# Pooled attention and a low-rank MLP on one core: a pair's remainders turned at once, outputs scaled on ScalarE, two adds a head given to GpSimd

## The chip, the cores and the metric

One core of one Trainium2 chip runs the whole program. The metric is the device time of one execution in microseconds. Three runs of the kernel before gave 885.32, 886.49 and 887.59 us, so the median is 886.49 us.

## The reference

The inputs are q, k and v of shape (4 batches, 8 heads, 1152 tokens, 64 columns) in float32, and the weights U, V, w_ch1 and w_ch2.

```
q_pool = q.reshape(B, H, S // 2, 2, D).mean(axis=3)          # 576 queries a head
scores = q_pool @ k^T / sqrt(D);  scores -= max over keys
attn   = exp(scores);  attn /= (sum over keys + 1e-09)
x      = attn @ v, heads side by side                        # (4, 576, 512)
h      = x^T @ U @ V        # along the tokens, rank 32
u      = x + h^T
out    = u + relu(u @ w_ch1) @ w_ch2                          # 512 -> 2048 -> 512
```

## The kernel before

There are 32 heads, numbered n = 8 b + h. The program does not write its instructions in their final order. It hands each piece of work to a planner (`Plan`, line 43) with a due time, the engines that may do it with a price in nanoseconds for each, and what it reads and writes. The planner runs a list schedule of its own prices: on each engine it takes the earliest due piece among those that can start soon enough (`SLACK`), and writes every engine's instructions in the order that comes out. On the chip each engine works through its own list in order. A piece with two engines (`dual`, line 399) goes to the one on which the planner sees it end first. VectorE pieces marked `port`, and all GpSimd pieces, are planned one after the other, and a link (line 1153) makes a GpSimd piece wait for the last VectorE piece of that kind.

A head goes through these steps, all in `head` (line 510). The pairs of query rows are added, turned and put in `Q1` and, for what the first rounding left, in `Q2`. The keys are turned into `T1`; a DMA copies T1 into `T2` and a row of ones lies beside it. Scans (line 696) multiply queries and keys once for a bound of each block's maximum, which VectorE reduces (line 702); the result is turned, negated and sent into a row of `Q2` by a DMA (line 731). Then the scores are computed again in the other orientation (lines 756 and 757), with keys in partitions: nine key blocks `j`, in three PSUM banks `s`. ScalarE takes the exponential of each bank into a unit of `big` (line 763). VectorE or GpSimd adds the units into `acc` (line 739): eight adds a head, seven in batch 0, whose last unit is summed by TensorE. TensorE multiplies the units with v into a bank of `m` (line 788), whose partitions 0 to 63 and 64 to 127 hold the head's outputs for the first and second 288 queries. Five banks `m` are shared by all that is not a score.

Every second head ends a pair. Each head's outputs are copied by ScalarE to `ay` (line 796), the pair's sums are formed by products with ones (line 779) and copied to `sr` (line 802). TensorE turns them by 128x128 products with an identity: three turns of the sums (line 825), four of the outputs' first 256 columns (`t4`) and two for the remaining 32 columns of each head, taken as the last 128 columns (`t2`, line 812). VectorE adds 1e-9 to the sums (line 828), takes reciprocals (line 832), multiplies the remainders into `XH` (line 835, two instructions) and the rest into `X` (line 839, one instruction of 512 columns).

After a batch's last head its `tail` (line 844) does the token mix and the MLP. Its products (lines 996, 1111 and 1040) are placed between the work of the next batch's heads, and after the last head TensorE does nothing else. In batch 0 there is no earlier MLP to place; while its heads run and after them, the weights are decoded (lines 430 to 438 and 920 to 923).

Of the kernel before, what the change touches and what calls it, by code (L numbers as in the profile page):

```python
# [9 lines left out]
F32 = mybir.dt.float32  # L10
# [3 lines left out]
AF = mybir.ActivationFunctionType  # L14
ALU = mybir.AluOpType
# [219 lines left out]
def kernel(  # L235
# [32 lines left out]
    FG = 2  # L268
    QT, KS = -9.86, -10.51
    LEAD = 52820.1, 7258.73  # L270
    WHOLE_KEYS, SPLIT = (False, False, True, True), 8
# [6 lines left out]
    LOOSE = (1, 0, 0, 0)  # L278
    SQUARES, SMALL = (False, False, True, True), 2.0
    APART = (True, True, False, False)  # L280
# [5 lines left out]
    SCALE = 0.5 / float(D) ** 0.5  # L286
    HEAD0, HEAD = 16770.0, 20724.3
    SLOT = HEAD / NG
    MLP_START, MLP_RATE = 5.082, (2.2, 2.197, 2.107, 2.2)
    DEC_START, DEC_LEAD = 98276.3, 12248.1  # L290
    SLACK = 18.29
    BIAS, BIAS_FROM = -300.0, 0.0
# [28 lines left out]
    def cut(of, first, n, shape, rows=P):  # L321
# [20 lines left out]
        acc=slots("acc", 3, [P, NQ]),  # L342
        ay=slots("ay", 2, [P, 2, HALF]),
        mp=slots("mp", 2, [P, 15]),
        mx=slots("mx", 2, [P, 5], F32R),
        mr=slots("mr", 2, [5, P], F32R),
        sr=slots("sr", 2, [P, HALF]),
        sm=slots("sm", 2, [P, 2, NS]),
# [50 lines left out]
    def dual(n, f):  # L399
        return {"dve": (v_(n), lambda: f(nc.vector)), "pool": (g_(n), lambda: f(nc.gpsimd))}  # L400
# [4 lines left out]
    def dma(nbytes):  # L405
        return nbytes / RATE

    def setup():
        nc.vector.memset(C["uh"][0].tile[:, 0, 0:2 * P].bitcast(F32), 1.0)
        make_identity(nc, ident)  # L410
        nc.vector.tensor_copy(identr, ident)
        for i in range(2):
            nc.gpsimd.memset(C["T2"][i].tile[D:D + 1].bitcast(F32), 1.0)
            nc.gpsimd.memset(C["mp"][i].tile, -3.0e38)
        nc.vector.memset(Vst[:, 0:PAD].bitcast(F32), 0.0)
        nc.gpsimd.memset(C["qb"][0].tile.bitcast(F32), 0.0)
# [93 lines left out]
    def head(n):  # L510
# [3 lines left out]
        T = lambda G: begin(n) + G * (SLOT if n >= NWHOLE else SLOT * HEAD0 / HEAD)  # L514
        whole = WHOLE_KEYS[b] and not SQUARES[b]
        kt, qt, vt, qp = (new(c) for c in ("k", "q", "v", "qp"))
        ks = None if whole else new("k" if SQUARES[b] else "ks")
        T1, T2, T3, Q1, Q2, qb, acc, mp = (new(c) for c in ("T1", "T2", "T3", "Q1", "Q2", "qb", "acc", "mp"))
        odd = h % 2
        if not odd:  # L520
            pair[:] = [new(c) for c in ("ay", "sr", "sm", "rs")] + [[], []]
        ay, sr, sm, rs, accs, summed = pair
        squares = SQUARES[b]
        if squares:
# [107 lines left out]
        if squares:  # L632
            kr = lambda: kt.t.rearrange("p j (x d) -> p (j x) d", d=32)
            kq = lambda: ks.t.rearrange("p j d -> p (j d)")
            for z in range(2):
                for c in range(2):
                    a = 32 * (2 * z + c)
                    op(T(-17), ("sp", SMALL * dma(73728), lambda a=a, z=z, c=c: nc.sync.dma_start(
                        kr()[a:a + 32], k[b, h, z * S // 2:(z + 1) * S // 2, 32 * c:32 * c + 32].rearrange("(m p) d -> p m d", p=32)), 0, 1200, BULK), go, [(kt, a)])
# [9 lines left out]
            t1, t3 = half_(0) + half_(1), [(T3, 0)]  # L649
            op(T(-6), ("act", 500, lambda: nc.scalar.dma_start(T2.t[0:D].bitcast(F32), T1.t[0:D].bitcast(F32)), 3300), [(T1, 0, 0), (T1, 1, 0)],  # L650
               [(T2, p_, z) for p_ in range(2) for z in range(2)])
# [10 lines left out]
        else:  # L662
# [19 lines left out]
            op(T(-6 if n else -20), way(lambda: que.dma_start(T2.t[0:D].bitcast(F32), T1.t[0:D].bitcast(F32)), 294912, 3300), t1, [(T2, p_, z) for p_ in range(2) for z in range(2)])  # L682
        op(T(-10), ("sp", dma(2 * 294912), lambda: nc.sync.dma_start(
# [54 lines left out]
        def add(at, a, b_, r):  # L738
            op(at, dual(NQ, lambda e: e.tensor_tensor(acc.t, a(), b_(), op=ALU.add)), r, [acc])  # L739

        for j in range(NJ):
            if j % 2 == 0:
                pair_ = j + 1 < NJ
                pu[j] = new("p2" if pair_ else "p1")
                if pair_:
                    pu[j + 1] = pu[j]
                    todo = [((j, j + 1), 0, NARROW, j), ((j,), NARROW, NQ, j + 0.9), ((j + 1,), NARROW, NQ, j + 1.493)]
                else:
                    todo = [((j,), 0, HALF, j), ((j,), HALF, NQ, j + 0.5)]
                for js, qa, qz, when in todo:  # L750
# [31 lines left out]
        for j0, j1 in GV[b]:  # L782
            last = j1 == NJ and odd and not APART[b]

            def value(js=range(j0, j1), last=last):
# [9 lines left out]
               [(vt, 0)] + keys(range(j0, j1)) + (summed if last else []), [pa] + ([pk] if last else []))  # L795
        op(T(NJ + AV), ("act", a_(HALF, True), lambda: nc.scalar.activation(ay.t[:, odd], pa.t[:, 0:HALF], AF.Copy)), [pa], [(ay, odd)])  # L796

        if not odd:
            return
        if APART[b]:  # L800
            op(T(NJ + AV), ("pe", parts * 4 * (HALF / 2.4 + 1.0) + TOT, total, TSL), summed, [pk])
        op(T(NJ + AV), ("act", a_(HALF, True), lambda: nc.scalar.activation(sr.t, pk.t[:, 0:HALF], AF.Copy)), [pk], [sr])

        first = (0, P, HALF - P)
        E = NJ + AV + YT
        pq, py, pz = new("m"), new("m"), new("m")
# [12 lines left out]
        def t2():
            for e in range(2):  # L820
                turn(e, HALF - P, pq.t[:, e * P:(e + 1) * P])

        def t3():
            for t, c0 in enumerate(first):
                nc.tensor.transpose(pz.t[:, t * P:(t + 1) * P], sr.t[:, c0:c0 + P], ident)

        op(T(E), ("pe", 3 * TP, t3), [sr], [pz])
        op(T(E + 0.1), ("dve", 80, lambda: nc.vector.tensor_scalar_add(
            sm.t, pz.t[:, 0:3 * P].rearrange("p (c e x) -> p e c x", e=2, x=32)[:, :, :, 0], 1e-9)), [pz], [sm])
        op(T(E), ("pe", 2 * TP, t2), [(ay, e) for e in range(2)], [pq])  # L830
        op(T(E), ("pe", 4 * TP, t4), [(ay, e) for e in range(2)], [py])
        op(T(E), ("dve", 135, lambda: nc.vector.reciprocal(rs.t, sm.t)), [sm], [rs])
        last = slice(P - 32, P)
        for f in range(2):
            op(T(E + 0.3), ("dve", v_(P) + 105, lambda f=f: nc.vector.tensor_tensor(
                XH[b].t[hb + 32 * f:hb + 32 * f + 32, cs].rearrange("p (e d) -> p e d", e=2),
                pq.t[last, 0:2 * P].rearrange("p (e f d) -> p f e d", e=2, f=2)[:, f],
                rs.t[last, :, 4 + f:5 + f].to_broadcast([32, 2, D]), op=ALU.mult)), [pq, rs], [(XH[b], b, h // 2, f)])
        op(T(E + 0.3), ("dve", v_(512), lambda: nc.vector.tensor_tensor(
            X[b].t[:, :, cs].rearrange("p t (e d) -> p t e d", e=2), py.t.rearrange("p (e t d) -> p t e d", e=2, d=D),  # L840
            rs.t[:, :, 0:4].rearrange("p e t -> p t e").unsqueeze(3).to_broadcast([P, 4, 2, D]), op=ALU.mult)),
           [py, rs] + (over if h > 1 else []), [(X[b], h // 2)] + (over if h == 1 else []))

    def tail(b, clock):
# [343 lines left out]
```

## Time and profile before

| | |
|---|---|
| median of the three runs | 886.49 us |
| profiled execution, its own time | 885.24 us |
| its span, first to last instruction | 883.1 us |
| TensorE busy | 872.8 us (99%) |
| VectorE busy | 751.9 us (85%) |
| ScalarE busy | 502.4 us (57%) |
| GpSimd busy | 218.8 us (25%) |

The profile shows one execution. Busy time of an engine is the time in which at least one of its instructions runs. Matmuls overlap and their ends are modelled, so a busy TensorE need not be at its peak. Two instructions that follow at once on VectorE or ScalarE overlap a little too. The chain that ended last follows the end of the program back to what released each step.

### The profile page before, as it was taken

The numbers are of one execution on the slowest core, as the hardware profiler recorded it, in microseconds if no ns is written. First come the engines' busy times: TensorE is split into PE (matmuls) and PEld (weight loads), VectorE is DVE, ScalarE is ACT, GpSimd is POOL, SyncE is SP. The second block draws the span as 40 slices with busy tenths as digits, with TensorE's granted clock in tenths as the row PEclk, the third lists the DMA queues.
The fourth block names the chain that finished last, engine by engine and source line by source line (L and its number), as shares of the span: only waits on it lengthen the run. The fifth ranks groups of instructions, "written<-read, shape, count | busy, mean of one in ns | idle before, by whom it ended". The sixth has DMA issues, their size and how long they took to land.

```text
span 883.1 us, 15648 instructions
## 1 busy us (share of the span) xinstructions
PE 872.8 (99%) x5469; PEld 710.0 (80%) x5469; DVE 751.9 (85%) x1494; ACT 502.4 (57%) x1094; POOL 218.8 (25%) x220
## 2 busy tenths in 40 slices
PE   9999999999999999999999999999999999999998
PEld 8777777687777777779888878888887788899987
DVE  8999999989999999997797889888884553898885
ACT  6788889767777777755454556455554221422220
POOL 2233332334344354550112122101130000111110
PEclk9999999999999999999999999999999999999999
DMA  5244364455657564883544545535442255455432
GB/s 171 80 125 147 90 180 142 130 170 191 220 165 223 167 156 135 225 209 89 150 105 100 140 94 126 126 80 149 112 146 85 96 184 195 173 193 190 167 104 100
DMA packets 146324, 128.73 MB, mean 146 GB/s; under 512 B 100907, under 2 KB 119110, under 8 KB 146246
## 3 DMA queue, kind: packets, MB, share of 16 engines
q1 hardware_dynamic: 143622, 118.47, 45.5%
q10 hardware_dynamic: 2624, 9.28, 4.4%
q8 instruction: 43, 0.70, 0.3%
q14 instruction: 35, 0.29, 0.1%
HBM read 96.17 MB, written 21.50 MB: 133 GB/s over the span
## 4 chain that ended last, share of the span: by engine, by line
PE 87%; DVE 8%; DMA 2%; ACT 2%; issue 1%; SPq 0%; ACTq 0%; DVEq 0%
PE m L1111 21%; PE m L996 15%; PE m L788 14%; PE s L756 7%; PE s L757 7%; PE m L696 7%; PE s L1040 6%; DVE mp L702 3%; DVE acc L739 1%; PE m L779 1%; DMA room<-mr 1%; PE m L812 1%; PE m L962 1%; PE m L669 1%; PE m L698 1%
## 5 line engine op out<-in xcount | busy, mean ns | idle before, releaser
L763 ACT ACTIVATE big<-s 128x320 f32<-128x320 f32 (+2 forms) x448 | 203.4, 479 | 127.0 <-PE s L757 124.2
L702 DVE TENSOR_REDUCE mp<-m 128x1 f32<-128x384 f32 (+1 forms) x448 | 216.2, 532 | 25.7 <-PE m L696 24.6
L1111 PE MATMUL m<-w,hh 128*128 128x512 f32 x798 | 223.9, 395 | 0.0
L996 PE MATMUL m<-rest,w 128*128 128x512 f32 (+1 forms) x768 | 186.1, 353 | 0.0
L756 PE MATMUL s<-room 128*128 128x256 f32 (+2 forms) x576 | 167.5, 302 | 0.7 <-ACT big L763 0.4
L757 PE MATMUL s<-room 65*128 65x256 f32 (+2 forms) x576 | 164.9, 298 | 1.8 <-DMA room<-mr 1.8
L1111 PEld LDWEIGHTS m<-w,hh 128*128 128x128 f32 x798 | 144.0, 188 | 23.1 <-ACT ay L796 0.5
L788 PE MATMUL m<-big,v 128*64 128x288 f32 x1152 | 148.5, 410 | 0.3 <-DVE mp L702 0.3
L996 PEld LDWEIGHTS m<-rest,w 128*128 128x128 f32 x768 | 132.8, 189 | 14.0 <-issue 1.4
L739 DVE TENSOR_TENSOR acc<-acc,big 128x576 f32<-128x576 f32 x162 | 125.2, 773 | 8.8 <-ACT big L763 6.8
L788 PEld LDWEIGHTS m<-big,v 128*64 128x64 f32 x1152 | 79.2, 137 | 58.7 <-issue 3.9
L696 PE MATMUL m<-room 128*128 128x384 f32 x384 | 125.6, 358 | 0.6 <-DVE mp L702 0.2
L756 PEld LDWEIGHTS s<-room 128*128 128x128 f32 x576 | 108.9, 189 | 13.0 <-issue 4.8
L757 PEld LDWEIGHTS s<-room 65*128 65x128 f32 x576 | 108.9, 189 | 8.3 <-issue 1.6
L739 POOL TENSOR_TENSOR acc<-acc,big 128x576 f32<-128x576 f32 x54 | 77.0, 1427 | 68.3 <-DVE acc L739 16.9
L696 PEld LDWEIGHTS m<-room 128*128 128x128 f32 x384 | 68.5, 188 | 19.5 <-DVE mp L702 4.7
L1115 DVE TENSOR_TENSOR X<-m,X 128x512 f32<-128x512 f32 x95 | 64.3, 681 | 12.0 <-PE m L1111 11.6
L438 POOL TENSOR_TENSOR wt<-wt,rx 128x512 int32<-128x512 int32 (+2 forms) x35 | 44.3, 1266 | 95.5 <-ACT big L763 20.7
L1002 DVE SCALAR_TENSOR_TENSOR hh<-m,hh 128x512 fp32r<-128x512 f32 (+1 forms) x64 | 37.4, 584 | 32.2 <-ACT hh L1000 31.8
L1000 ACT ACTIVATE hh<-m 128x512 fp32r<-128x512 f32 (+1 forms) x64 | 32.9, 514 | 52.3 <-PE m L996 51.6
L584 POOL CAST qb<-room 64x64 fp32r<-64x64 f32 x50 | 16.4, 329 | 135.4 <-DVE acc L739 42.0
L394 ACT ACTIVATE room<-m 64x288 fp32r<-64x288 f32 (+1 forms) x109 | 46.3, 438 | 2.0 <-PE m L570 0.5
(137 smaller groups left out, 1055.8 us busy)
## 6 DMA issues: line engine op xcount, KB each, us to landing
w<-wc SPq DMA_DIRECT2D x96, 512.0 KB
rx<-in_moe_w_ch_dram SPq DMA_DIRECT2D x32, 512.0 KB
wc<-w SPq DMA_DIRECT2D x32, 512.0 KB
v<-in_v_dram SPq DMA_DIRECT2D x32, 288.0 KB
room<-room ACTq DMA_DIRECT2D x31, 288.0 KB
q<-in_q_dram SPq DMA_DIRECT2D x16, 288.0 KB
k<-in_k_dram SPq DMA_DIRECT2D x64, 72.0 KB
q<-in_q_dram SPq DMA_DIRECT2D x128, 36.0 KB
```

The costliest lines, as they stand in the source:

```text
L394: ways = {"act": (a_(n, True) + hold, lambda: f(lambda o, i: nc.scalar.activation(o, i, AF.Copy)), far)}
L696: nc.tensor.matmul(pm.t[:, 0:w], Q1.t[:, t * P - 64:t * P + 64], T1.t[:, cs_], start=True, stop=True)
L702: op(T(MX0 + 0.3 + MXS * u / 14), ("dve", v_(w), lambda c=c, t=t, w=w, pm=pm: nc.vector.reduce_max(mp.t[:, c * 5 + t:c * 5 + t + 1], pm.t[ ...
L739: op(at, dual(NQ, lambda e: e.tensor_tensor(acc.t, a(), b_(), op=ALU.add)), r, [acc])
L756: nc.tensor.matmul(o, T1.t[:, kc], Q1.t[:, qa:qz], start=True, stop=False)
L757: nc.tensor.matmul(o, T2.t[:, kc], Q2.t[:, PAD + qa:PAD + qz], start=False, stop=True)
L763: op(T(when + 0.1), ("act", a_(len(js) * nq, True), lambda js=js, qa=qa, qz=qz, nq=nq, ss=ss, p=pu[j], e=js[0] % 2: nc.scalar.activation(p ...
L788: nc.tensor.matmul(pa.t[hf * D:(hf + 1) * D, 0:HALF], vt.t[:, j], pu[j].t[:, j % 2, hf * HALF:(hf + 1) * HALF], start=(j == 0), stop=(j == ...
L996: op(now, ("pe", mm(nb), lambda c=c, i=i, a=a, bb=bb, w=w, ph=ph, sl=sl: nc.tensor.matmul(ph.t[:, 0:nb], w.t[:, a, c * P:(c + 1) * P], (ul ...
L1040: nc.tensor.matmul(bank.t[:, 0:NB], left(a, c), ub.t[:, i, bb, c], start=(c == 0 and j == 0), stop=(c == 1 and j == 2))
L1111: op(now, ("pe", mm(512), lambda f=f, i=i, a=a, bb=bb, w=w, h_=h_: nc.tensor.matmul(po.t, h_.t[:, a, ns], w.t[:, bb], start=(f == fg and i ...
L1115: op(now, ("dve", v_(512), lambda: nc.vector.tensor_tensor(x(), po.t, x(), op=ALU.add)), [po], bk[t])
```

## The change

For each pair, `ay` becomes one row of 864 columns: the first 256 columns of head 0, of head 1 and of the sums, then the last 32 columns of each of the three. ScalarE copies each of the three sources in two pieces (`keep`). Seven turns follow: two for the sums and one for all three remainders at once (`t3`), and four for the outputs (`t4`). The added 1e-9 takes three instructions for one, and the multiplications of the remainders become four pieces of 64 columns that may go to ScalarE or VectorE. In batches 0 and 1 (`SCALED`) the rest of the outputs is scaled on ScalarE, two pieces of four activations with a scale for each partition, in place of one VectorE multiplication. In heads 0 to 15 (`GIVEN`) the adds of units 1 and 2 go to GpSimd and all others to VectorE. `SQUARES` changes its form only: it held for batches 2 and 3 and now holds from head 16. Several due times and promised landing times move.

```diff
-    QT, KS = -9.86, -10.51
-    LEAD = 52820.1, 7258.73
+    QT, KS = -9.86, -10.14
+    LEAD = 68186.1, 7053.71
+    SCALED = (True, True, False, False)
+    SQUARES, SMALL = 16, 2.0
+    GIVE, GIVEN = (1, 2), 16
-    HEAD0, HEAD = 16770.0, 20724.3
+    HEAD0, HEAD = 16680.3, 20724.3
-    MLP_START, MLP_RATE = 5.082, (2.2, 2.197, 2.107, 2.2)
-    DEC_START, DEC_LEAD = 98276.3, 12248.1
-    SLACK = 18.29
+    MLP_START, MLP_RATE = 5.082, (2.2, 2.197, 2.131, 2.099)
+    DEC_START, DEC_LEAD = 80776.6, 12248.1
+    SLACK = 16.65
-        ay=slots("ay", 2, [P, 2, HALF]),
+        ay=slots("ay", 2, [P, 6 * P + 96]),
-        sr=slots("sr", 2, [P, HALF]),
+        for x in C["sm"]:
+            nc.gpsimd.memset(x.tile, 1.0)
...
-  k's loads of batches 2 and 3:  ... .rearrange("(m p) d -> p m d", p=32)), 0, 1200, BULK), go, [(kt, a)])
+  k's loads of batches 2 and 3:  ... .rearrange("(m p) d -> p m d", p=32)), 0, 1800, BULK), go, [(kt, a)])
-  both copies of T1 into T2:     ... nc.scalar.dma_start(T2.t[0:D].bitcast(F32), T1.t[0:D].bitcast(F32)), 3300)
+  both copies of T1 into T2:     ... nc.scalar.dma_start(T2.t[0:D].bitcast(F32), T1.t[0:D].bitcast(F32)), 4300)
...
         def add(at, a, b_, r):
-            op(at, dual(NQ, lambda e: e.tensor_tensor(acc.t, a(), b_(), op=ALU.add)), r, [acc])
+            ways = dual(NQ, lambda e: e.tensor_tensor(acc.t, a(), b_(), op=ALU.add))
+            if n < GIVEN:
+                ways = {"pool": ways["pool"]} if j in GIVE else {"dve": ways["dve"]}
+            op(at, ways, r, [acc], port=True)
...
-                    todo = [((j, j + 1), 0, NARROW, j), ((j,), NARROW, NQ, j + 0.9), ((j + 1,), NARROW, NQ, j + 1.493)]
+                    todo = [((j, j + 1), 0, NARROW, j), ((j,), NARROW, NQ, j + 0.8295), ((j + 1,), NARROW, NQ, j + 1.493)]
-                    todo = [((j,), 0, HALF, j), ((j,), HALF, NQ, j + 0.5)]
+                    todo = [((j,), 0, HALF, j), ((j,), HALF, NQ, j + 0.3653)]
...
-        op(T(NJ + AV), ("act", a_(HALF, True), lambda: nc.scalar.activation(ay.t[:, odd], pa.t[:, 0:HALF], AF.Copy)), [pa], [(ay, odd)])
+        def keep(e, src):
+            op(T(NJ + AV), ("act", a_(2 * P, True), lambda: nc.scalar.activation(ay.t[:, 2 * e * P:2 * (e + 1) * P], src.t[:, 0:2 * P], AF.Copy)), [src], [(ay, e)])
+            op(T(NJ + AV), ("act", a_(32, True) + 16, lambda: nc.scalar.activation(
+                ay.t[:, 6 * P + 32 * e:6 * P + 32 * (e + 1)], src.t[:, 2 * P:HALF], AF.Copy)), [src], [(ay, "last", e)])
+        keep(odd, pa)
...
-        op(T(NJ + AV), ("act", a_(HALF, True), lambda: nc.scalar.activation(sr.t, pk.t[:, 0:HALF], AF.Copy)), [pk], [sr])
+        keep(2, pk)
-        pq, py, pz = new("m"), new("m"), new("m")
+        py, pz = new("m"), new("m")
...
         def t3():
-            for t, c0 in enumerate(first):
-                nc.tensor.transpose(pz.t[:, t * P:(t + 1) * P], sr.t[:, c0:c0 + P], ident)
+            for i in range(2):
+                turn(4 + i, pz.t[:, i * P:(i + 1) * P])
+            nc.tensor.transpose(pz.t[0:96, 2 * P:3 * P], ay.t[:, 6 * P:], ident)
-        op(T(E), ("pe", 2 * TP, t2), [(ay, e) for e in range(2)], [pq])
+        for e in range(2):
+            op(T(E + 0.1), ("dve", 110, lambda e=e: nc.vector.tensor_scalar_add(
+                sm.t[32 * e:32 * e + 32, 0, 4:6], pz.t[64:96, 2 * P:3 * P].rearrange("p (f e x) -> p e f x", e=2, x=32)[:, e, :, 0], 1e-9)),
+               [pz], [(sm, e)])
...
         for f in range(2):
-            op(T(E + 0.3), ("dve", v_(P) + 105, lambda f=f: nc.vector.tensor_tensor(... pq, rs ...)), [pq, rs], [(XH[b], b, h // 2, f)])
+            for e in range(2):
+                op(T(E + 0.3), {
+                    "act": (a_(D, True) + MOVE, lambda to=to, fr=fr, by=by: nc.scalar.activation(to(), fr(), AF.Copy, scale=by())),
+                    "dve": (v_(D) + 105, lambda to=to, fr=fr, by=by: nc.vector.tensor_scalar(to(), fr(), by(), None, op0=ALU.mult)),
+                }, [pz, rs], [(XH[b], b, h // 2, f, e)])
+        if SCALED[b]:
+            for e in range(2):
+                def scaled(e=e):
+                    for t in range(4):
+                        nc.scalar.activation(X[b].t[:, t, (h - 1 + e) * D:(h + e) * D], py.t[:, 2 * e * P + t * D:2 * e * P + (t + 1) * D], AF.Copy, scale=rs.t[:, e, t:t + 1])
+                op(T(E + 0.3), ("act", 4 * (a_(D, True) + 16), scaled), [py, rs] + (over if h > 1 else []), [(X[b], h // 2, e)] + (over if h == 1 and e == 1 else []))
+        else:
+            the VectorE multiplication of 512 columns as before
```

## Rows read from the trace of the kernel before

**Rows 1.** The page: busy time of each engine, and tenths in 40 slices.

```profile
PE 872.8 (99%) x5469; PEld 710.0 (80%) x5469; DVE 751.9 (85%) x1494; ACT 502.4 (57%) x1094; POOL 218.8 (25%) x220
...
PE   9999999999999999999999999999999999999998
...
DVE  8999999989999999997797889888884553898885
ACT  6788889767777777755454556455554221422220
```

**Rows 2.** The page: shares of the chain that ended last, by engine.

```profile
PE 87%; DVE 8%; DMA 2%; ACT 2%; issue 1%; SPq 0%; ACTq 0%; DVEq 0%
```

**Rows 3.** Stages: us, busy (x instructions) of PE, PEld, DVE, ACT, POOL, clock, DMA.

```profile
19.40:140.20 120.80, 119.75 (x887) 90.90 (x886) 115.78 (x255) 100.36 (x236) 38.89 (x43) 1.00 0.45 127
140.20:178.30 38.10, 35.98 (x249) 26.03 (x242) 37.61 (x74) 31.97 (x73) 10.42 (x9) 1.00 0.44 133
178.30:332.20 153.90, 152.82 (x920) 119.71 (x919) 144.29 (x283) 112.31 (x239) 66.44 (x54) 1.00 0.62 187
332.20:700.00 367.80, 366.13 (x2363) 300.70 (x2362) 306.97 (x596) 201.65 (x438) 80.80 (x81) 1.00 0.50 127
700.00:883.00 183.00, 179.97 (x921) 155.48 (x919) 131.57 (x255) 44.54 (x87) 15.71 (x16) 1.00 0.47 163
```

**Rows 4.** The chain within 19.4 to 140.2 us, shares by line.

```profile
by line: PE m L788 23.1%; PE s L756 13.3%; PE s L757 12.4%; PE m L696 12.0%; DVE mp L702 7.5%; DVE acc L739 4.8%; ACT room L394 3.6%; issue 2.9%; PE m L669 2.8%; PE m L779 2.5%; DMA room<-mr 2.0%; PE m L698 1.6%; PE m L812 1.6%; ACT big L76
```

**Rows 5.** Timelines and chain: start us, us, engine, line, what, count: dense TensorE work.

```profile
61.79 0.28 PE L756 MATMUL s<-room 128*128 128x256 f32 x1
61.91 0.29 PE L757 MATMUL s<-room 65*128 65x256 f32 x1
62.03 0.69 PE L696 MATMUL m<-room 128*128 128x384 f32 x3
62.56 0.31 PE L756 MATMUL s<-room 128*128 128x320 f32 x1
62.70 0.31 PE L757 MATMUL s<-room 65*128 65x320 f32 x1
62.85 0.34 PE L696 MATMUL m<-room 128*128 128x384 f32 x1
...
24.05 3.06 PE m L788 x24
...
49.82 0.27 PE L812 MATMUL m<-ident,ay 128*128 128x128 f32 x1
...
697.16 0.60 PE L812 MATMUL m<-ident,ay 128*128 128x128 f32 x4
```

**Rows 6.** ScalarE's forms: count, busy us, mean ns of one, idle before.

```profile
L796 ACT ACTIVATE ay<-m 128x288 f32<-128x288 f32 x32 | 13.2, 411 | 41.6 <-PE m L788 41.5
L939 ACT ACTIVATE room<-m 128x256 fp32r<-128x256 f32 x5 | 1.9, 378 | 0.0
L938 ACT ACTIVATE room<-m 128x128 fp32r<-128x128 f32 x5 | 1.4, 278 | 4.8 <-PE m L962 4.8
```

**Rows 7.** Line 739's adds by stage: us, busy (x) of DVE, of POOL.

```profile
0.00:140.00 140.00, 37.71 (x50) 8.51 (x6) 1.00 0.46 131
140.00:332.00 192.00, 33.07 (x43) 30.02 (x21) 1.00 0.58 176
```

**Rows 8.** Forms of VectorE and GpSimd: count, busy us, mean ns of one.

```profile
L835 DVE TENSOR_TENSOR XH<-m,rs 32x128 f32<-32x128 f32 x32 | 9.4, 295 | 1.1
L839 DVE TENSOR_TENSOR X<-m,rs 128x512 f32<-128x512 f32 x12 | 8.3, 691 | 0.4
L828 DVE TENSOR_SCALAR sm<-m 128x12 f32<-128x12 f32 x16 | 2.6, 160 | 7.5 <-PE m L825 7.5
L936 DVE TENSOR_TENSOR wt<-m,wt 128x128 f32<-128x128 f32 x15 | 3.4, 279 | 0.0
L739 POOL TENSOR_TENSOR acc<-acc,big 128x576 f32<-128x576 f32 x54 | 77.0, 1427 | 68.3 <-DVE acc L739 16.9
```

More of the change, by code (lines that the diff above doesn't have):

```diff
@@ L278 @@
     LOOSE = (1, 0, 0, 0)
-    SQUARES, SMALL = (False, False, True, True), 2.0
+    SCALED = (True, True, False, False)
+    SQUARES, SMALL = 16, 2.0
+    GIVE, GIVEN = (1, 2), 16
     APART = (True, True, False, False)
@@ L514, in head @@
         T = lambda G: begin(n) + G * (SLOT if n >= NWHOLE else SLOT * HEAD0 / HEAD)
-        whole = WHOLE_KEYS[b] and not SQUARES[b]
+        whole = WHOLE_KEYS[b] and not (n >= SQUARES)
         kt, qt, vt, qp = (new(c) for c in ("k", "q", "v", "qp"))
-        ks = None if whole else new("k" if SQUARES[b] else "ks")
+        ks = None if whole else new("k" if (n >= SQUARES) else "ks")
         T1, T2, T3, Q1, Q2, qb, acc, mp = (new(c) for c in ("T1", "T2", "T3", "Q1", "Q2", "qb", "acc", "mp"))
@@ L520, in head @@
         if not odd:
-            pair[:] = [new(c) for c in ("ay", "sr", "sm", "rs")] + [[], []]
-        ay, sr, sm, rs, accs, summed = pair
-        squares = SQUARES[b]
+            pair[:] = [new(c) for c in ("ay", "sm", "rs")] + [[], []]
+        ay, sm, rs, accs, summed = pair
+        squares = (n >= SQUARES)
         if squares:
@@ L638, in head @@
                     op(T(-17), ("sp", SMALL * dma(73728), lambda a=a, z=z, c=c: nc.sync.dma_start(
-                        kr()[a:a + 32], k[b, h, z * S // 2:(z + 1) * S // 2, 32 * c:32 * c + 32].rearrange("(m p) d -> p m d", p=32)), 0, 1200, BULK), go, [(kt, a)])
+                        kr()[a:a + 32], k[b, h, z * S // 2:(z + 1) * S // 2, 32 * c:32 * c + 32].rearrange("(m p) d -> p m d", p=32)), 0, 1800, BULK), go, [(kt, a)])
             op(T(KS + 0.5), ("dve", v_(S // 2), lambda: nc.vector.transpose(kq(), kt.t.rearrange("p j d -> p (j d)"))), [(kt, 32 * a) for a in range(4)], [ks])
@@ L649, in head @@
             t1, t3 = half_(0) + half_(1), [(T3, 0)]
-            op(T(-6), ("act", 500, lambda: nc.scalar.dma_start(T2.t[0:D].bitcast(F32), T1.t[0:D].bitcast(F32)), 3300), [(T1, 0, 0), (T1, 1, 0)],
+            op(T(-6), ("act", 500, lambda: nc.scalar.dma_start(T2.t[0:D].bitcast(F32), T1.t[0:D].bitcast(F32)), 4300), [(T1, 0, 0), (T1, 1, 0)],
                [(T2, p_, z) for p_ in range(2) for z in range(2)])
@@ L681, in head @@
                    t1[0:2] if z == 0 else t1[1:], [(T3, z)])
-            op(T(-6 if n else -20), way(lambda: que.dma_start(T2.t[0:D].bitcast(F32), T1.t[0:D].bitcast(F32)), 294912, 3300), t1, [(T2, p_, z) for p_ in range(2) for z in range(2)])
+            op(T(-6 if n else -20), way(lambda: que.dma_start(T2.t[0:D].bitcast(F32), T1.t[0:D].bitcast(F32)), 294912, 4300), t1, [(T2, p_, z) for p_ in range(2) for z in range(2)])
         op(T(-10), ("sp", dma(2 * 294912), lambda: nc.sync.dma_start(
@@ L801, in head @@
             op(T(NJ + AV), ("pe", parts * 4 * (HALF / 2.4 + 1.0) + TOT, total, TSL), summed, [pk])
-        op(T(NJ + AV), ("act", a_(HALF, True), lambda: nc.scalar.activation(sr.t, pk.t[:, 0:HALF], AF.Copy)), [pk], [sr])
-        first = (0, P, HALF - P)
+        keep(2, pk)
         E = NJ + AV + YT
-        pq, py, pz = new("m"), new("m"), new("m")
+        py, pz = new("m"), new("m")
         over = [("raw", "use")] if b == 2 else []
@@ L809, in head, with turn @@
         hb = 64 * par
-        def turn(e, c0, out):
-            nc.tensor.transpose(out, ay.t[:, e, c0:c0 + P], ident)
+        def turn(i, out):
+            nc.tensor.transpose(out, ay.t[:, i * P:(i + 1) * P], ident)
         def t4():
-            for e in range(2):
-                for t in range(2):
-                    turn(e, t * P, py.t[:, (2 * e + t) * P:(2 * e + t + 1) * P])
-        def t2():
-            for e in range(2):
-                turn(e, HALF - P, pq.t[:, e * P:(e + 1) * P])
@@ L823, in t3 @@
-        def t3():
-            for t, c0 in enumerate(first):
-                nc.tensor.transpose(pz.t[:, t * P:(t + 1) * P], sr.t[:, c0:c0 + P], ident)
-        op(T(E), ("pe", 3 * TP, t3), [sr], [pz])
-        op(T(E + 0.1), ("dve", 80, lambda: nc.vector.tensor_scalar_add(
-            sm.t, pz.t[:, 0:3 * P].rearrange("p (c e x) -> p e c x", e=2, x=32)[:, :, :, 0], 1e-9)), [pz], [sm])
-        op(T(E), ("pe", 2 * TP, t2), [(ay, e) for e in range(2)], [pq])
-        op(T(E), ("pe", 4 * TP, t4), [(ay, e) for e in range(2)], [py])
@@ L832, in head @@
[L832 to L842, printed above, removed]
+            for i in range(4):
+                turn(i, py.t[:, i * P:(i + 1) * P])
+        def t3():
+            for i in range(2):
+                turn(4 + i, pz.t[:, i * P:(i + 1) * P])
+            nc.tensor.transpose(pz.t[0:96, 2 * P:3 * P], ay.t[:, 6 * P:], ident)
@@ new lines, in head @@
+        op(T(E), ("pe", 3 * TP, t3), [(ay, 2)] + [(ay, "last", e) for e in range(3)], [pz])
+        op(T(E + 0.1), ("dve", 80, lambda: nc.vector.tensor_scalar_add(
+            sm.t[:, :, 0:4], pz.t[:, 0:2 * P].rearrange("p (c e x) -> p e c x", e=2, x=32)[:, :, :, 0], 1e-9)), [pz], [(sm, 2)])
+        for e in range(2):
+            op(T(E + 0.1), ("dve", 110, lambda e=e: nc.vector.tensor_scalar_add(
+                sm.t[32 * e:32 * e + 32, 0, 4:6], pz.t[64:96, 2 * P:3 * P].rearrange("p (f e x) -> p e f x", e=2, x=32)[:, e, :, 0], 1e-9)),
+               [pz], [(sm, e)])
@@ new lines, in head @@
+        op(T(E), ("pe", 4 * TP, t4), [(ay, e) for e in range(2)], [py])
+        op(T(E), ("dve", 135, lambda: nc.vector.reciprocal(rs.t, sm.t)), [(sm, e) for e in range(3)], [rs])
+        for f in range(2):
+            for e in range(2):
+                r0 = slice(32 * e, 32 * e + 32)
+                to = lambda e=e, f=f: XH[b].t[hb + 32 * f:hb + 32 * f + 32, (h - 1 + e) * D:(h + e) * D]
+                fr = lambda r0=r0, f=f: pz.t[r0, 2 * P + f * D:2 * P + (f + 1) * D]
+                by = lambda r0=r0, f=f: rs.t[r0, 0, 4 + f:5 + f]
+                op(T(E + 0.3), {
+                    "act": (a_(D, True) + MOVE, lambda to=to, fr=fr, by=by: nc.scalar.activation(to(), fr(), AF.Copy, scale=by())),
+                    "dve": (v_(D) + 105, lambda to=to, fr=fr, by=by: nc.vector.tensor_scalar(to(), fr(), by(), None, op0=ALU.mult)),
+                }, [pz, rs], [(XH[b], b, h // 2, f, e)])
@@ new lines, in head @@
+        if SCALED[b]:
+            for e in range(2):
+                def scaled(e=e):
[3 more added lines that the diff above has]
+        else:
+            op(T(E + 0.3), ("dve", v_(512), lambda: nc.vector.tensor_tensor(
+                X[b].t[:, :, cs].rearrange("p t (e d) -> p t e d", e=2), py.t.rearrange("p (e t d) -> p t e d", e=2, d=D),
+                rs.t[:, :, 0:4].rearrange("p e t -> p t e").unsqueeze(3).to_broadcast([P, 4, 2, D]), op=ALU.mult)),
+               [py, rs] + (over if h > 1 else []), [(X[b], h // 2, e) for e in range(2)] + (over if h == 1 else []))
@@ L855, in hkeys @@
         def hkeys(t):
-            return [k for i in range(H // 2) for k in ([(X[b], i)] if t < 4 else [(XH[b], b, i, f) for f in range(2)])]
+            return [k for i in range(H // 2) for e in range(2) for k in ([(X[b], i, e)] if t < 4 else [(XH[b], b, i, f, e) for f in range(2)])]
         now = begin((b + 1) * H) + MLP_START * SLOT
@@ L879, in tail @@
         for c in range(1, 3):
-            op(now, ("sp", dma(65536), lambda c=c: nc.sync.dma_start(tr()[c * R:(c + 1) * R], tr()[0:R]), 175), [(trow, 0)], [(trow, c)])
+            op(now, ("sp", dma(65536), lambda c=c: nc.sync.dma_start(tr()[c * R:(c + 1) * R], tr()[0:R]), 175, 1300), [(trow, 0)], [(trow, c)])
         op(now, ("act", a_(DM), lambda: nc.scalar.activation(ts(), tr(), AF.Copy)), [(trow, c) for c in range(4)], [(z, "s")])
```

## Prediction

> **What bounds the kernel now.** I began with the busy line and the slices [rows 1]. TensorE is busy 872.8 of 883.1 us, and its digit is 9 nearly everywhere, so at first sight only removed TensorE work counts. But a busy TensorE there includes modelled ends. The slices also show VectorE at 8 or 9 for the first 16 slices (to about 350 us), ScalarE at 5 to 8 there, and both falling later. The chain that ended last [rows 2] has 87% on TensorE and 8%, some 70 us, on VectorE: waits too short to open a gap in TensorE's row, but in the path.
>
> The table by stage [rows 3] tells where. The cuts are the first adds of heads 0, 8 and 16 (19.4, 140.2 and 332.2 us), the end of the fill after batch 0 (178.3), and the last head's end (700). In batch 0 VectorE is busy 115.8 of 120.8 us (96%), ScalarE 100.4 (83%), GpSimd 38.9 (32%). From 178 to 332 VectorE has 94%, from 332 to 700 83%. In batch 0's own chain [rows 4] VectorE's two lines 702 and 739 have 12.3%, nearly 15 us.
>
> How much of batch 0 TensorE could give up follows from its dense rates [rows 5]: 0.12 us for 256 columns of scores (61.79 to 61.91), 0.145 for 320 (62.56 to 62.70), (0.69 - 0.34)/2 = 0.175 for a scan of 384, 3.06/24 = 0.1275 for a value product, (0.60 - 0.27)/3 = 0.11 for a pair's turn. (0.34 and 0.27 are the durations of one scan, at 62.85, and of one turn, at 49.82.) A head of batch 0 has 16 + 16 scores and 4 of 288 (4.8 us), 36 values (4.6), 12 scans and 2 short ones (2.4), and 12 turns of q and k, sums and half a pair's turns (estimated together 2.0 from the turn's 0.11): 13.8 us. Eight make 110 of the stage's 120.8. So some 10 us there are TensorE waiting in small pieces, the upper bound of what relieving the others can return. Later stages have MLP products to put between.
>
> **The change, part by part.** The sum is made on the profiled execution, 885.24 us (span 883.1 and 2.1 around it); the median of the three runs, 886.49, is 1.25 above it.
>
> 1. Turns, 9 to 7 a pair. Two fewer at 0.11 us is 0.22 us; 16 pairs, 3.5 us of TensorE. The seventh turn has 96 columns as weights but still streams 128 columns, so I price it like the others. In batches 1 to 3 TensorE is the path: 12 x 0.22 = **-2.6 us**. Batch 0's 0.9 us goes into step 4, because it falls where TensorE waits anyway. One bank fewer of the five "m" is taken for a pair; no row shows a wait for it, so nothing.
>
> 2. ScalarE. An output or sum was copied at once, 411 ns for 288 columns; now 256 columns (378 by the form of line 939) and 32. Forms of 128 and 256 columns (278 and 378) give 0.78 ns a column, so 32 cost about 203 and 64 about 228 [rows 6]. Copies: 3 x (378 + 203 - 411) = +0.51 us a pair, in all batches. In batches 0 and 1 a pair's outputs are scaled by eight instructions of 64 columns: 8 x 228 = 1.82 us, with ends 8 x 203 = 1.6 and 8 x 278 = 2.2. The remainder's four scalings go to ScalarE or VectorE as the planner finds them free: 0 to 4 x 278 = 1.1 us, I take 0.5. Together +2.8 us a pair (2.1 to 3.8); four pairs bring batch 0's ScalarE from 100.4 to 112 (109 to 116), 90 to 96% of the old stage.
> No row has an activation whose scale is read from memory, and all the new scalings are of this kind. The Trainium skill ("ScalarE: Activation LUTs", section "What ACT_TABLE_LOAD costs") says that each such pointer operand adds about 93 ns. By that rule ten scalings a pair would put another 3.7 us on batch 0, near 116 us in all, and this speaks against the change. No run here shows it yet.
>
> 3. VectorE. In batch 0 GpSimd had 6 of 56 adds, after the change 16 (two a head): VectorE loses 10 x 37.71/50 = 7.5 us. In batch 1 GpSimd had 21 of 64, after 16: VectorE gets 5 x 33.07/43 = +3.8 [rows 7]. Per pair of batches 0 and 1 the multiply of 691 ns goes; the two remainder multiplies (590 ns) become four of 64 columns, about 213 ns each between the 160 of 12 columns and the 279 of 128 [rows 8], of which I give VectorE half, 0.43 (0 to 0.85); the sums' reciprocals get two more small adds, 2 x 0.16. That is -0.69 - 0.59 + 0.43 + 0.32 = -0.53 us, four times -2.1. Batch 0: -9.6, so 115.8 becomes 106. Batch 1: +3.8 - 2.1 = +1.7. In batches 2 and 3, -0.59 + 0.43 + 0.32 = +0.16 us a pair, at 83% busy: nothing.
>
> 4. What batch 0 gives. TensorE needs 110 - 1, VectorE 106, ScalarE 112: the longest is 112 instead of VectorE's 115.8. If the stage keeps the 5.0 us that VectorE left free, it ends at 117, a gain of 3.8. Bounds: nothing (ScalarE takes VectorE's place in full) and -9.6 (VectorE's whole relief). ScalarE's work comes in lumps, so I take **-2.5 us**. For batch 1 the bounds are -0.5 and +1.7; I take **+0.5**, since MLP products cover most of it.
>
> 5. Forced adds. The third add of a head now waits, on VectorE, for GpSimd's second; behind it stand the maxima of the next head's scans, and behind these TensorE's "m" banks. GpSimd needs 1427 ns an add [rows 8] and the planner reckons 2.127 x 576 + 207 = 1432, so the written order should have it done in time. GpSimd's batch 0 goes from 38.9 to 38.9 + 10 x 1.42 = 53 us of 120.8, so it is free most of the time. I take 0; if each of the 16 heads waited one GpSimd add, it would be 23 us, so this cover matters. Two more memsets at the start lie under the first loads.
>
> 6. Moved due times and longer promised landings (k 1800 for 1200, the copy of T1 into T2 4300 for 3300 ns) make the planner put dependents later. The chain gives all DMA 2% [rows 2], some 18 us, of which I expect nothing in either direction; bounds -2 and +2, from the eight or so single waits of this kind that could move by a quarter microsecond each.
>
> Sum: -2.6 - 2.5 + 0.5 = -4.6 us. From 886.49 that is **881.9**; I say 881.5, since step 1's part in batch 0 is not quite nothing.
>
> **The rivals.**
> *Whole relief.* VectorE's 9.6 us in batch 0 come back entire: -9.6 - 2.6 = 874. For it: lines 702 and 739 in that stage's chain. Against it: TensorE's own 109 us and ScalarE's 112 let the stage shrink by hardly more than 9.
> *Absorbed.* ScalarE is the new limit of batch 0 and the five adds returned in batch 1 cost 1.7: -2.6 + 1.7, near 885.5. For it: ScalarE's 83% before 2.8 us or more a pair. Against it: 112 is still less than 115.8.
> *Slower: the score banks wait for ScalarE.* Its place is heads 0 to 15. Exponentials drain three "s" banks, which TensorE fills in 0.48 + 0.29 + 0.29 = 1.06 us. If a pair's eight scalings run back to back, ScalarE is away for 1.82 us and TensorE stands 0.76 us, 8 pairs 6.1 us. With no relief in batch 0: -2.6 + 6.1 + 1.7 = +5.2, 891.7. It decides once scalings exceed 1.06 us without an exponential between them, and without scans or value products ready. For it: in-order ScalarE, and the two groups become ready at the same moment. Against it: they are two groups that the planner may part, and in [rows 4] no ScalarE line but the query copies of line 394 weighs much.
> A rival that the change doesn't do what it says I hold out for the adds alone: they might have sat with GpSimd in the stage where it matters already; the 6 of 56 exclude that.
> The Trainium skill ("SBUF — State Buffer", section "SBUF: two separate sides") says that GpSimd and VectorE lock a shared port pair, so that the loser blocks for the whole instruction. By it ten adds moved in batch 0 lock the pair for 14 us to free 7.5 of VectorE, and the relief could be void, which is the absorbed case. The kernel links its turns on that port itself, so the rows before do not show a blocked instruction; VectorE's maxima read PSUM and can run meanwhile.
>
> **How the numbers follow.** About 0.3%, 2.7 us, is what a measurement of this kernel can tell from no change: faster is under 883.8, slower over 889.2. Forecast (878 to 883.8) 0.50, whole relief (872 to 878) 0.15, absorbed (to 889) 0.23, slower 0.12. Faster 0.65, same 0.23, slower 0.12. The range 873 to 889.5 leaves out some 0.04 below and 0.11 above.
>
> **What would show it.** Seven turns a pair at 0.11 us; first adds of heads 0 and 8 closer together than 120.8 us; VectorE near 88% and ScalarE above 90% in that stretch; GpSimd with 32 adds before head 16. The whole relief would show in a batch 0 under 113 us, the slower case in TensorE waiting for exponentials of line 763 just after the scalings. The prediction is wrong if batch 0 does not shorten, or if the gain sits after head 16, where I count only turns.

## The result, and the profile after

The changed kernel took 894.33 us (median of five, 891.51 to 896.14), the kernel before 886.49: ratio 1.0090, interval 1.0078 to 1.0103. It is slower by 7.8 us; 881.5 was forecast. Experiments are given by their ratio to runs of the kernel before on the same chip, whose medians lay between 885.7 and 886.5.

The page of the profiled execution (896.14 us, span 894.4) against [rows 1]:

```profile
PE 880.0 (98%) x5437; PEld 712.2 (80%) x5437; DVE 751.4 (84%) x1513; ACT 526.4 (59%) x1248; POOL 222.7 (25%) x217
...
PEclk9999989999999999999999999999999999999999
```

TensorE has 32 matmuls fewer and is busy 7 us longer. One slice of the granted clock is not 9; before, all were:

```profile
PEclk9999999999999999999999999999999999999999
```

The profiled execution is the slowest of the five. In it batch 0, between the first adds of heads 0 and 8, runs from 21.1 to 149.0 us, where it was 19.4 to 140.2 before (columns as in [rows 3]):

```profile
21.10:149.00 127.90, 124.33 (x871) 93.34 (x873) 115.91 (x250) 107.90 (x282) 52.70 (x51) 0.96 0.45 131
```

The stage takes 127.9 us for 120.8. VectorE is busy as long as before (115.9 for 115.8), GpSimd 14 us longer and ScalarE 7.5 us longer. No engine is the bound (TensorE apart, whose busy time holds modelled ends), and the stage is late. Where it got late is seen at the first exponential and where the last value products of heads 7 and 15 start (start us, us, what). Before:

```profile
16.19 0.59 ACT L763 ACTIVATE big<-s 128x512 f32<-128x512 f32 x1
...
134.14 1.68 PE L788 MATMUL m<-big,v 128*64 128x288 f32 x12
...
322.74 4.59 PE L788 MATMUL m<-big,v 128*64 128x288 f32 x36
```

After:

```profile
17.88 0.59 ACT L769 ACTIVATE big<-s 128x512 f32<-128x512 f32 x1
...
143.57 1.68 PE L794 MATMUL m<-big,v 128*64 128x288 f32 x12
...
333.45 4.59 PE L794 MATMUL m<-big,v 128*64 128x288 f32 x36
```

Head 7's last values are 9.4 us late. Of this 1.7 us stand before the first exponential and are not the change's: two versions below with the same order have their first exponential at 15.92 and at 17.67 us, so the start varies from one execution to another. That leaves 7.7 us lost in batch 0, 1.3 more in batch 1 and 0.5 later. The chain that ended last shows how, at the end of a pair of batch 0 (start us, us, what):

```profile
115.82 0.24 DVE rs L841
...
116.15 0.30 ACT XH L849
...
116.46 0.30 ACT XH L849
...
116.78 0.31 ACT XH L849
...
117.11 1.75 ACT X L856 x8
118.87 0.50 ACT big L769
119.36 0.04 issue
119.41 0.56 PE s L762
```

Eleven scalings, 2.7 us, stand on ScalarE without an exponential between them. TensorE's side of it:

```profile
118.02 0.37 PE L701 MATMUL m<-room,qb 128*128 128x288 f32 x1
118.92 0.40 PE L701 MATMUL m<-room,qb 128*128 128x288 f32 x1 [0.52 <-ACT X L856]
119.41 0.56 PE L762 MATMUL s<-room 128*128 128x256 f32 x1
119.77 0.42 PE L763 MATMUL s<-room 65*128 65x256 f32 x1
```

The second short scan starts 0.90 us after the first, the score 0.49 after that, and then a score of 256 columns takes 0.21 us for 0.12: the clock is at its lower level. TensorE's waits for ScalarE from 19 to 144 us (us in total, times, longest us) are of two kinds:

```profile
PE m L701 <- ACT X L856: 1.3, 2, 0.8
PE s L762 <- ACT big L769: 1.0, 1, 1.0
```

Twice, here and at 86.4 us, the scan waits for the last of eight scalings. By the program it can only be waiting for a bank `m`: the turned outputs lie in one of the five until they are scaled. The other wait, at 55.3 us, is a score's for a bank `s`, which an exponential had not yet drained, and so is one of 1.3 us at 155.4 us, behind batch 0's last pair. Three stretches at the lower clock in the table by windows (clock in the third column from the right):

```profile
88.70:92.20 3.50, 3.50 (x16) 1.76 (x16) 3.44 (x8) 2.85 (x6) 0.00 (x0) 0.51 0.02 7
...
119.40:126.30 6.90, 6.89 (x29) 4.97 (x31) 5.92 (x11) 4.74 (x11) 2.16 (x2) 0.51 0.07 26
...
157.00:160.40 3.40, 3.40 (x17) 2.56 (x18) 3.40 (x7) 2.97 (x10) 0.00 (x0) 0.50 0.00 1
```

Each begins 0.6 to 2.3 us after a pair's scalings; together they are 13.8 us at 1.2 instead of 2.4 GHz, at most 6.9 us of work. The pair at 55.3 us had its wait and no such stretch.

The forms that answer to [rows 6] and [rows 8]:

```profile
L803 ACT ACTIVATE ay<-m 128x256 f32<-128x256 f32 x48 | 18.5, 386 | 52.0 <-PE m L794 50.8 <-PE m L785 0.5
L856 ACT ACTIVATE X<-m,rs 128x64 f32<-128x64 f32 x64 | 14.2, 327 | 0.2
L849 ACT ACTIVATE XH<-m,rs 32x64 f32<-32x64 f32 x41 | 12.5, 306 | 7.6 <-DVE rs L841 5.2 <-DVE XH L850 1.8
L804 ACT ACTIVATE ay<-m 128x32 f32<-128x32 f32 x48 | 9.5, 198 | 0.0
...
L850 DVE TENSOR_SCALAR XH<-m,rs 32x64 f32<-32x64 f32 x23 | 6.3, 274 | 1.4 <-ACT XH L849 1.0
L837 DVE TENSOR_SCALAR sm<-m 32x2 f32<-32x2 f32 x32 | 5.0, 155 | 0.4
```

One scaling lasts 327 ns, and 64 of them occupy 14.2 us, 222 ns each, since neighbours overlap. The planner reckons 0.833 x 64 + 51 + 16 = 120.

### The profile page after: what moved, and what is told of

Its sections match the earlier page's. It is cut to its first block, busy times and chain, and to the rows that moved or that the text cites. A ratio compares the mean times of both kernels' runs of the same rounds, so it can differ in the third digit from the quotient of the medians.

```text
span 894.4 us, 15750 instructions
## 1 busy us (share of the span) xinstructions
PE 880.0 (98%) x5437; PEld 712.2 (80%) x5437; DVE 751.4 (84%) x1513; ACT 526.4 (59%) x1248; POOL 222.7 (25%) x217
## 4 chain that ended last, share of the span: by engine, by line
PE 80%; DVE 12%; ACT 5%; DMA 2%; issue 1%; SPq 0%; ACTq 0%; DVEq 0%
PE m L1131 19%; PE m L794 15%; PE m L1016 14%; PE s L762 7%; PE s L763 6%; PE m L699 6%; PE s L1060 6%; DVE mp L705 4%; DVE acc L742 2%; ACT X L856 2%; DMA room<-mr 1%; PE m L672 1%; DVE X L1135 1%; PE m L785 1%; PE m L891 1%
## 5 line engine op out<-in xcount | busy, mean ns | idle before, releaser
L762 PE MATMUL s<-room 128*128 128x256 f32 (+2 forms) x576 | 170.6, 307 | 2.8 <-ACT big L769 2.3
L794 PE MATMUL m<-big,v 128*64 128x288 f32 x1152 | 152.2, 417 | 0.0
L742 DVE TENSOR_TENSOR acc<-acc,big 128x576 f32<-128x576 f32 x172 | 135.7, 789 | 13.5 <-ACT big L769 10.9
L742 POOL TENSOR_TENSOR acc<-acc,big 128x576 f32<-128x576 f32 x44 | 62.8, 1427 | 47.8 <-ACT big L769 29.5
L1135 DVE TENSOR_TENSOR X<-m,X 128x512 f32<-128x512 f32 x95 | 64.4, 682 | 10.4 <-PE m L1131 10.0
L803 ACT ACTIVATE ay<-m 128x256 f32<-128x256 f32 x48 | 18.5, 386 | 52.0 <-PE m L794 50.8
```

The lines of the kernel that those rows point to most:

```text
L742: ways = dual(NQ, lambda e: e.tensor_tensor(acc.t, a(), b_(), op=ALU.add))
L762: nc.tensor.matmul(o, T1.t[:, kc], Q1.t[:, qa:qz], start=True, stop=False)
L794: nc.tensor.matmul(pa.t[hf * D:(hf + 1) * D, 0:HALF], vt.t[:, j], pu[j].t[:, j % 2, hf * HALF:(hf + 1) * HALF], start=(j == 0), stop=(j == ...
L1135: op(now, ("dve", v_(512), lambda: nc.vector.tensor_tensor(x(), po.t, x(), op=ALU.add)), [po], bk[t])
```

## The experiments

Theory A: scales read from memory hold ScalarE longer than the planner reckons, exponentials come late, TensorE waits and its clock falls. B: the forced adds hold VectorE. C: the moved due times. D: ScalarE's wait for the reciprocals. E: any newly planned order costs time.

**The same order, scales as constants** (the reciprocals are not applied)

```
-  AF.Copy, scale=rs.t[:, e, t:t + 1])      and  scale=by()
+  AF.Copy, scale=0.5)                           scale=0.5
```

> The changed kernel, every engine's order unchanged, but the 105 activations that scale outputs take a constant 0.5 written in the instruction in place of a scale read from memory (so they read no reciprocals and wait for none; the outputs are left unscaled by the sums). Theory A (a scale read from memory costs ScalarE some 100 ns an instruction that the planner did not reckon, the exponentials come late at a pair's end in heads 0 to 15, TensorE runs dry and its clock then falls): one such activation of 64 columns takes 215 to 235 ns for 327, no stretch at half clock in batch 0, and 883 to 888 us. Rival B (adds forced on GpSimd hold VectorE) and rival C (the moved due times make a worse order by themselves): the order is the same, so 892 to 896 us, and the clock still falls.

882.14 us, ratio 0.9956 (0.9944 to 0.9968), just under the range expected: 12 us come back with every engine's order unchanged. B and C by themselves fall.

```profile
L849 ACT ACTIVATE XH<-m 32x64 f32<-32x64 f32 x41 | 8.7, 213 | 4.8 <-PE m L699 2.0 <-DVE XH L850 1.8 <-DVE sm L837 0.5
L856 ACT ACTIVATE X<-m 128x64 f32<-128x64 f32 x64 | 8.5, 247 | 0.2
```

```profile
110.23 0.67 ACT L849 ACTIVATE XH<-m 32x64 f32<-32x64 f32 x3
110.92 1.04 ACT L856 ACTIVATE X<-m 128x64 f32<-128x64 f32 x8
111.77 1.34 ACT L769 ACTIVATE big<-s 128x512 f32<-128x512 f32 x3
```

```profile
core 0: 880.4 us, clock 1.000
```

```profile
19.10:140.00 120.90, 118.84 (x871) 90.32 (x873) 112.47 (x250) 104.87 (x282) 52.74 (x51) 1.00 0.46 139
```

```profile
15.92 0.59 ACT L769 ACTIVATE big<-s 128x512 f32<-128x512 f32 x1
...
134.60 1.68 PE L794 MATMUL m<-big,v 128*64 128x288 f32 x12
...
320.44 4.59 PE L794 MATMUL m<-big,v 128*64 128x288 f32 x36
```

The eight scalings take 1.04 us for 1.75 (a scaling occupies 133 ns, not 222), no stretch at the lower clock is left before the last microsecond, and head 7's last values start 9.0 us earlier than after the change, 7.0 if both are counted from the first exponential. The values that go into X are others, but batch 0's time is already different before its mix reads them.

**Constants in the outputs' 64 scalings alone**, the remainders' kept

> The changed kernel in its own order; only the 64 scalings of outputs on ScalarE (line 856) take a constant in the instruction (outputs of batches 0 and 1 left unscaled); the remainders' 41 keep the scale read from memory and with it the wait for the reciprocals. The run before, with all 105 changed, also took away ScalarE's waits for the reciprocals (5.2 us at the remainders). Theory A (the price of a read scale): 882 to 886 us, most of the 12 us are back. Rival D (the wait for the reciprocals is what holds ScalarE): 890 to 895 us.

884.45 us, 0.9989 (0.9979 to 0.9999): 9 (by the ratios) to 9.9 (by the medians) of the 12 us. The remainders still wait for the reciprocals here, so D falls; the 41 remainders have the other 2 to 3.

**Constants in batch 0 alone** (`scale=... if b else 0.5`)

> The changed kernel in its own order, with constants in the scalings of batch 0 alone (outputs of batch 0 left unscaled); from batch 1 on scales are read from memory. Theory A by place: by the last value product of head 7 the changed kernel was 8.9 us behind the version with constants everywhere, by that of head 15 13 us; so 884 to 887 us. If the loss sat in batch 1: 889 us or more.

885.67 us, 1.0000 (0.9991 to 1.0009): 8 to 8.7 of the 12 us, in the stage where the prediction looked for its gain.

**The kernel before with read scales in its 48 copies**

```
-  nc.scalar.activation(ay.t[:, odd], pa.t[:, 0:HALF], AF.Copy)
+  nc.scalar.activation(ay.t[:, odd], pa.t[:, 0:HALF], AF.Copy, scale=ones[:, 0:1])      # and for sr
```

> The kernel before in its own order, but its 48 copies of outputs and sums on ScalarE (lines 796 and 802) take a scale of one read from memory: nothing else is changed and the result is the same. Theory A's price by itself: the copies take 500 to 510 ns for 411, ScalarE's work grows by 48 x 0.095 = 4.6 us, and 885.5 to 889 us, since before had ScalarE at 83% and the copies stand alone. If a read scale costs nothing: 411 ns and no change.

```profile
L796 ACT ACTIVATE ay<-m,ones 128x288 f32<-128x288 f32 x32 | 16.0, 501 | 41.3 <-PE m L788 41.2
L802 ACT ACTIVATE sr<-m,ones 128x288 f32<-128x288 f32 x16 | 8.0, 501 | 1.6 <-PE m L779 0.4
```

501 ns for 411, so the price is 90 ns; yet 886.14 us, 1.0004 (0.9996 to 1.0012). On copies that stand alone it is covered; on eight or eleven scalings in a row it is not.

**Nine turns in the version with constants** (the sums' two turns done twice, order unchanged)

```
-  for i in range(2):
+  for i in (0, 1, 0, 1):
```

> The version with constants in the scalings (882.1 us), its order unchanged, with the two turns of a pair's sums done twice: nine turns again, 32 more of 0.11 us. If turns are on the path as the prediction had it (2.6 us outside batch 0): 884.3 to 885.9 us. If they fall into waits: 882 to 883 us.

884.67 us against 882.14: by the medians 2.5 us for 32 turns, where the prediction had 2.6. The fastest runs of the two (883.50 and 882.09) differ by 1.4 us. The two profiled executions differ by 2.8 us in their spans, but 1.75 of these lie before the first exponential (17.67 us here), which leaves 1.1. So turns are on the path, at a price between 1.1 and 2.5 us.

**Outputs multiplied by VectorE** (`SCALED` off; planned anew, as are all that follow)

> The changed kernel with outputs of batches 0 and 1 multiplied by VectorE as before (SCALED off), all else as changed, planned anew. Theory A: ScalarE loses 64 x 222 ns, 14 us, before head 16 and VectorE gains 8 x 0.69 us; no stretch at half clock; 882 to 888 us. Rivals B and C: 891 to 896 us.

884.09 us, 0.9974 (0.9963 to 0.9985). It leaves nothing out and beats both kernels: the one before by 2.4 us, the change by 10.

**And the remainders on VectorE alone**

> The changed kernel with outputs multiplied by VectorE and the remainders' four multiplications on VectorE alone, planned anew: no activation with a scale from memory is left. Theory A: no worse than the version that left the remainders to either engine (884.1), 880 to 885 us. If VectorE is as tight as before, 885 to 889 us.

894.96 us, 1.0104. A miss: no read scale is left on ScalarE, and it is slow. Its longest TensorE wait is elsewhere, 4.3 us for the row of maxima:

```profile
PE s L763 <- DMA room<-mr: 5.8, 3, 4.3
```

**Adds left to the planner** (`GIVEN` 0)

> The changed kernel with the adds of heads 0 to 15 left to the planner again (GIVEN 0), outputs still scaled on ScalarE, planned anew. Rival B: 884 to 888 us. Theory A and rival C: 891 to 897 us, with TensorE waits behind the scalings and the clock fallen at least once.

904.75 us, 1.0209, above every range expected. The opposite of B: without the forced adds it is 10 us slower still, though in another order.

**Scalings at a truer price in the plan** (four for 988, a remainder's for 306 ns)

> The changed kernel with the planner's price of a scaling corrected: four of them 988 ns for 481, one of the remainder's 306 for 234; planned anew. Theory A: the planner parts the scalings or puts scans and values beside them; the work stays, so 884 to 891 us. Rivals B and C: 891 to 896 us.

895.97 us, 1.0115. A miss: knowing the price, the planner finds nothing better. So a right price in the plan is not shown to be a cure.

**Seven turns alone**, with the new due times

> The changed kernel with neither part for batches 0 and 1 (outputs multiplied by VectorE, adds left to the planner), so seven turns and the new due times alone, planned anew. If the forced adds are what gave 884.1 us against 886.5: 885 to 890 us here. If the seven turns gave it: 882 to 885 us.

896.0 us, 1.0110. Its longest wait of TensorE is again elsewhere:

```profile
PE m L910 <- DVE xs L903: 2.5, 1, 2.5
```

**and with the old**

> The same with the due times, promised landings and slack of the kernel before: only the seven turns and their copies are changed. Turns on the path: 882 to 885 us. Rival C (due times make the difference): it would stand 3 us or more away from the run with the new times.

895.17 us, 1.0102. Both miss: what the turns give is buried under some 10 us or more of a new order, with old and new times alike.

**The kernel before, slack moved**

> The kernel before with the planner's slack alone moved, 18.29 to 16.65 ns: the same instructions, planned anew in another order. Theory E (any new order of this kernel costs time until its due times fit it again): 888 to 898 us. If an order is worth little by itself: 885 to 888 us.

885.26 us, 0.9995 (0.9986 to 1.0004). It says little on E, because its order is nearly the old one: in the traces 1091 of ScalarE's 1094 instructions and 1492 of VectorE's 1494 stand in the same sequence. For the next version these are 903 and 1209.

**The kernel before, pace of the first heads moved** (16770.0 to 16680.3)

> The kernel before with the pace of the first heads alone moved, 16770.0 to 16680.3 ns a head: the same work, planned anew. Theory E: 888 to 898 us. If an order is worth little by itself, or the faster pace was a gain: 883 to 888 us.

894.31 us, 1.0102 (1.0088 to 1.0117): the same work, 8.6 us slower. The largest piece is one wait of the mix after batch 1:

```profile
PE m L890 <- DVE xs L883: 4.3, 2, 4.0
```

E holds for this order.

**The whole change with the old due times**

> The whole change (seven turns, scalings, forced adds) with the due times, promised landings and slack of the kernel before, planned anew. Theory A: the scalings cost it too, 892 us or more. Rival C (the moved due times did it): 882 to 888 us.

892.61 us, 1.0076 (1.0064 to 1.0088). With the old due times it is slow too, so the moved ones are not needed to make it slow. As E alone would give such a time, the run does not speak for A.

**GpSimd scales** (ScalarE copies outputs in two pieces of 256 columns, GpSimd multiplies them in X)

```
+  op(T(E + 1.3), ("pool", g_(2 * P), lambda: nc.gpsimd.tensor_tensor(xe(), xe(), <reciprocals spread over 64>, op=ALU.mult)), ...)
```

> A version meant to keep the relief without the price: in batches 0 and 1 ScalarE copies a pair's outputs unscaled into X in two activations of 256 columns for eight of 64, and GpSimd multiplies X in place by the reciprocals, two instructions of 256 columns a pair; planned anew. ScalarE loses eight times 0.22 us a pair and gets back two times 0.27. Theory A: 880 to 886 us if the new order is a good one. Theory E (a new order costs by itself): 888 to 896 us.

893.2 us, 1.0078 (1.0061 to 1.0095). No better than the change. Of the nine versions whose order was written anew (all but the slack's) eight took 892.6 to 904.8 us; only outputs multiplied by VectorE did not.

## Why the prediction was wrong, by its steps

Step 1 (turns): the kind was right, and a fixed order shows it; the size is at most right, 1.1 to 2.5 us for all 32 turns where 2.6 was reckoned for 24 of them. It also put the banks `m` at nothing, because no row showed a wait for one; after the change TensorE waits for one behind the scalings, 0.8 and 0.5 us in the trace.

Step 2 (ScalarE): the copies were right (386 and 198 ns for 378 and 203). A scaling was not: 327 ns for 228, over the upper end of 278, because that end came from activations with constants. The rule named there holds: the Trainium skill ("ScalarE: Activation LUTs", section "What ACT_TABLE_LOAD costs") has about 93 ns for such an operand, and the runs give 90 (501 for 411) and, in what a scaling occupies of ScalarE, 89 (222 for 133). The amount for eight, 1.82 us, came out nearly right (1.75) by two errors that cancel: neighbours overlap by some 0.1 us, which I did not take off.

Step 3 (VectorE): the adds went as reckoned, the relief did not. Between the first adds of heads 0 and 8 VectorE was to fall from 115.8 to 106 us; it stood at 115.9, and at 112.5 with constants. Some 2 us went into adds that overlap a GpSimd instruction (0.95 to 1.9 us for 0.75, five in this stage, four with constants, none before). About 3.5 us are pieces of the weights' decoding (lines 435 to 439 and 941), which the change starts earlier. GpSimd had 16 adds in batch 0 and 16 in batch 1:

```profile
0.00:142.00 142.00, 29.68 (x38) 22.80 (x16) 0.96 0.45 132
142.00:342.00 200.00, 40.38 (x50) 22.80 (x16) 0.99 0.57 170
```

Step 4 is the one that failed: "ScalarE's work comes in lumps, so I take -2.5 us". Batch 0 lost 7.1 us between the first adds of heads 0 and 8 (127.9 for 120.8), outside the bounds of nothing and -9.6. I compared busy sums, 112 against 115.8, and by sums ScalarE had room, as it still has after (107.9 of 127.9 us, 84%). What decides is where the lump stands. The planner placed eight scalings as 0.96 us (8 x 120); they take 1.75, a remainder's 0.31 for 0.234. The bank `m` that they read and the exponentials queued behind are late by that at the end of each of batch 0's four pairs. Step 5 held the planner's price of a GpSimd add (1432) against the trace (1427) and found the order safe. The same comparison for a scaling, 481 ns in the plan for four against the 912 that step 2 reckons, would have cast doubt on the order; I did not make it.

The rival "the score banks wait for ScalarE" was near to this mechanism, at 891.7 us and a chance of 0.12. It had the place right and the price of a wait (0.76 us; 0.5 to 1.3 in the trace). It named the wrong bank for two of the four pairs, where an `m` bank and not a score bank held TensorE, and all eight pairs, where of batch 1's four only the last shows a wait of this size (0.7 us). It lacked the clock: after three of the four TensorE ran 3.4 to 6.9 us at half its rate. Of the changed kernel's five runs two had a mean clock of 0.996 (891.5 and 893.1 us), three 0.992 (894.3 to 896.1). So one such share of 0.004, some 7 us at half rate, goes with about 3 us, and of the 12 us roughly half are the clock's (an estimate from these five runs) and half the waits. Up to head 7's last values two stretches, 10.4 us at half rate, account for up to 5.2 of the 7.7 us, and the three waits for 2.3.

Even with the price taken away the gain is not the one forecast. In that version head 7's last values start 0.5 us later than before, 0.7 from the first exponential: batch 0, where VectorE's relief was 3 us and not 10, gave nothing. The gain over the kernel before sits in batch 1, 2.8 us between heads 7 and 15, where I expected a loss of 0.5 and, from four pairs' turns, a gain of 0.9; what gave the rest is not shown. After head 15, where eight pairs' turns were to bring 1.8 us, the version is only 0.5 us ahead. That its 882.1 us meet the forecast of 881.5 is chance.

Rival C (due times) and B (adds) do not explain the change. What stays open is why newly planned orders without eight scalings in a row on ScalarE, or with the kernel before's own work, also land at 893 to 896 us. Each of the three shown has another long wait. What they share is that the clock falls around such waits: the traces have 6.8 us at 1.2 GHz with all scaling on VectorE (from 376.7 us), 13.7 and 6.8 with the turns alone (new and old times), 6.8 with the moved pace, where before has none until its end. At half rate 6.8 us cost at most 3.4 of the some 9 us lost, and why a new order brings these waits is not explained. So the gain of a part can be read here only between versions in one order.

## What to carry to other kernels

Where an order is written from prices, hold each new instruction's price against a trace before counting busy time: an engine with room to spare still stops its neighbours when a run of small instructions is longer than planned. Here the corrected price alone did not give a good order (895.97 us); taking the run off ScalarE did in one order (884.09) and not in another (894.96). A scale read from memory costs 90 ns an activation, which disappears among others and adds up in a run. To learn what one part costs, change it without changing the order; a version planned anew can mix in some 10 us of its own. Before stages of two profiles are compared, count them from the same event: here 1.7 us of the difference lay before the first exponential.

## What the runs showed of the hardware

After three of four waits of TensorE at the ends of batch 0's pairs (0.8, 0.5 and 1.3 us) its clock was at 1.2 GHz for 3.4 to 6.9 us; after the fourth (1.0 us) and after one of 0.8 us in the version with constants it stayed at 2.4. The kernel before and the version with constants have no such stretch until the end. An activation of 64 columns lasts 247 ns with a constant scale and 327 with one from memory, and of ScalarE's time it occupies 133 and 222: eight in a row take 1.04 and 1.75 us. VectorE's adds that overlap a GpSimd instruction last up to 1.9 us, where the others take 0.75.
